# Linear attention and a Mish feed-forward layer: transposes of query features and x moved from TensorE to VectorE and device memory

## The chip, the cores and the metric

The kernel runs on one core of a Trainium2 chip. The metric is device time in microseconds (us) of one execution. The time before the change is 1163.37 us, the median of 3 runs (1163.05 to 1163.79). The profiled execution that all views below show took 1165.86 us, with a span of 1164.1 us between the first and the last instruction.

## What is computed

First comes an attention with positive features, for 8 batches, 8 heads, 576 positions and head size 64. Its result, as 4608 rows of 512, goes through a feed-forward layer with 2048 inner columns.

```python
def phi(x):
    proj = np.einsum('bhsd,df->bhsf', x, w_phi)
    proj = proj - np.max(np.abs(proj), axis=-1, keepdims=True)
    return np.concatenate([np.exp(proj), np.exp(-proj)], axis=-1)
q_p, k_p = (phi(q), phi(k))
kv = np.einsum('bhsf,bhsd->bhfd', k_p, v)
z = np.sum(k_p, axis=2)
num = np.einsum('bhsf,bhfd->bhsd', q_p, kv)
den = np.einsum('bhsf,bhf->bhs', q_p, z)[..., None] + 1e-06
x = (num / den)        # then rows of B*S by columns of H*D
h = x @ w_in
sp = np.where(h > 20.0, h, np.log1p(np.exp(np.minimum(h, 20.0))))
g = h * np.tanh(sp)    # Mish
return (g @ w_out).astype(np.float32)
```

## The kernel before

**The work.** The 4608 rows are 18 chunks `c` of 256. A chunk has two query units `q{c}_{g}` (g = 0, 1: two pairs of heads each), so there are 36 of them. The keys are 36 units `k{n}` of 512 rows, loaded five units ahead of the queries.

A key unit is projected (`project`, L241), which gives two tiles `pp` of 128 positions x 128 features for four blocks; VectorE subtracts the largest absolute value (`centre`, L249: two reductions into `m`, two subtractions into `e[:, 0]`); ScalarE takes the two exponentials (`k_exp`, L289); and TensorE adds features times values into `kvps` (`k_sum`, L294). Positions stand on the partitions there, which is what the sum over positions needs.

A query unit starts the same way, but its product with `kv` sums over features, so features have to stand on the partitions. In `q_turn` (L313) TensorE therefore transposes the centred features of each `j` (0, 1) in four 128x128 blocks into a PSUM tile `dt`, and `q_exp` (L319) reads the exponentials from there. `q_num` (L324) makes the products `num`, `q_divide` (L335) divides them by their last column into `x`, and `q_out` (L345) transposes `x` in four blocks into the PSUM tile `xt`, since the feed-forward layer again needs columns of x on the partitions. `q_high` (L352) and `q_low` (L356) split that into a rounded part `xTh` and a rest `xTl`. So a query unit has twelve 128x128 transposes on TensorE: three groups of four, two in `q_turn` and one in `q_out`.

The feed-forward layer of a chunk has 16 tiles `f` of 128 inner columns. `ff_in` (L366) makes `h` of a tile with 12 matmuls of 256 columns. Two tiles share one PSUM bank; there are two such banks (pool `h`). For each pair of tiles ScalarE applies Mish into `u` and rounds it into `gh` (`mish`, L379; the bank is free once `u` is written), VectorE takes the rest `gl` (L388), and `ff_out` (L401) adds six matmuls of 512 columns per tile into the output tiles `o`, some four tiles behind `ff_in`.

**What sets the order.** `Plan` holds every step as a task with an engine, a key (its due time, counted in tiles `f`), an assumed duration, the tasks that it depends on and the buffers that it takes and gives back. `order` (L57) plays them through and writes down the order in which each engine issues them. On the chip each engine follows that order strictly: an instruction that waits holds up everything behind it on its engine, and so does a DMA that waits on SyncE (SP). From the seventh query unit on (`NFIRST = 6`) a new query unit and a new key unit start every 8 tiles: a *step*. In a step, TensorE does, in this order, the sum of the old key unit and `num` of the old query unit, then `project` of the next query and key unit, among `ff_in` and `ff_out` in turn.

ScalarE computes Exp and Mish from two function tables; each change costs an `ACT_TABLE_LOAD`.

Of the kernel before, what the change touches and what calls it, by code (L numbers as in the profile page):

```python
# [8 lines left out]
F32 = mybir.dt.float32  # L9
# [7 lines left out]
P = 128  # L17
# [5 lines left out]
CH = 256  # L23
# [8 lines left out]
PARTS = ((4, 8, 16), (4, 8, 16))  # L32
NSUMMED = 16

NK, LEAD = B * NHP * S // 512, 5
LEADIN = 5
FIRST_KEYS = {0: -14.0, 1: -13.0, 2: -12.0, 3: -11.0, 4: -10.0, 5: 5.0, 6: 7.0, 7: 9.0, 8: 10.0, 9: 26.0, 10: 30.0}
FIRST_QUERIES = {0: -9.0, 1: -8.0, 2: -2.0, 3: -1.0, 4: 11.0, 5: 12.5}
NFIRST = 6
E0, E1, GX = 0.27, 0.36, 0.6  # L40
WKEYS = [-7.0, -6.0, -5.0, -4.0, -1.5, -0.5, 0.5, 1.5, 3.0, 3.5, 4.0, 4.5, 7.5, 8.0, 8.5, 9.0]
# [4 lines left out]
class Plan:  # L46
# [3 lines left out]

    def add(self, name, engine, key, took, fn, deps=(), take=(), give=(), late=0.15, table=None, size=0):
        task = dict(name=name, engine=engine, key=key, took=took, fn=fn, deps=deps, take=take, give=give, late=late,
                    table=table, size=size, seq=len(self.tasks))
        self.tasks.append(task)
        self.named[name] = task

    def order(self, held):  # L57
# [8 lines left out]

        def ready(task):
            for dep in task["deps"]:
# [52 lines left out]
def attention_then_mish(ctx, tc, qT, kT, va, w_phi, w_in, w_out, out):  # L121
# [39 lines left out]
    def bank(kind, shape, name):  # L161
        return banks[kind].tile(shape, F32, tag=kind, name=name)
# [103 lines left out]
    def halves(ps, lhsT, rhs, start, stop):  # L266

        for h in range(2):
            rows = slice(h * D, (h + 1) * D)
            nc.tensor.matmul(ps[rows], lhsT[:, rows], rhs[h], start=start, stop=stop, skip_group_check=True)  # L270

# [38 lines left out]

    turned, nums, x_live, xT, xt_ps = {}, {}, {}, {}, {}

# [6 lines left out]
    def q_exp(c, g, j):  # L319
        e, ps = features[f"q{c}_{g}"][j], turned.pop((c, g, j))  # L320
        for s in range(2):
            nc.scalar.activation(e[:, s, :], ps, AF.Exp, scale=2.0 * s - 1.0)  # L322

    def q_num(c, g, i):  # L324
        es = features[f"q{c}_{g}"]
        ps = nums[c, g, i] = bank("att", [P, 2, 2, VW], f"num{i}_{c}_{g}")
        for t in range(2):
            r0 = (2 * c + t) * P
            for j in range(2):
                for s in range(2):  # L330
                    halves(ps[:, t, j], es[j][:, s, (2 * i + t) * P:(2 * i + t + 1) * P],
                           [kv[(r0 + h * D) // S, 2 * g + i][:, j, s] for h in range(2)],
                           start=(t == j == s == 0), stop=(s == 1))

    def q_divide(c, g, i):  # L335
        ps = nums.pop((c, g, i))
        if i == 0:
# [5 lines left out]
                                r.unsqueeze(3).broadcast_to([P, 2, 2, D]), op=ALU.mult)  # L343

    def q_out(c, g):  # L345
        x = x_live.pop((c, g))
        ps = xt_ps[c, g] = bank("att", [P, 2, CH], f"xt_{c}_{g}")
        for i in range(2):
            for t in range(2):
                nc.tensor.transpose(ps[:, i, t * P:(t + 1) * P], x[:, i, t], ident)  # L350

    def q_high(c, g):  # L352
        hi = moe.tile([P, 2, CH], F32R, tag="xTh", name=f"xTh_{c}_{g}", bufs=NXT)
        nc.scalar.copy(hi, xt_ps[c, g])  # L354
        xT[c, g] = (hi, None)

    def q_low(c, g):
        hi = xT[c, g][0]
        lo = moe.tile([P, 2, CH], F32R, tag="xTl", name=f"xTl_{c}_{g}", bufs=NXT)
        nc.vector.tensor_sub(lo, xt_ps.pop((c, g)), hi.bitcast(F32))  # L360
        xT[c, g] = (hi, lo)
# [71 lines left out]


    add = plan.add
    key_time = dict(FIRST_KEYS)
    query_time = dict(FIRST_QUERIES)
    for n in range(NFIRST, 2 * NCH):
        query_time[n] = 8.0 * n - 18.0
        if n + LEAD < NK:  # L440
            key_time[n + LEAD] = 8.0 * n - 18.0

    def unit_tasks(unit, t, load, src, kinds, size):
        home, homes = raw_home(), [e_home(), e_home()]
# [5 lines left out]
        for h in homes:  # L450
            last_use.setdefault(h, []).append(f"sum {unit}" if unit[0] == "k" else f"num {unit} 1")
        add(f"project {unit}", "PE", t, 1.0, lambda: project(unit, kinds), deps=[f"load {unit}"],
            take=[(kind, f"pp{j}:{unit}") for j, kind in enumerate(kinds)], give=[token] if half != 0 else [])
# [3 lines left out]
    shared_by, last_use = {}, {}  # L457
    units = sorted([(t, 0, n) for n, t in key_time.items()] + [(t, 1, n) for n, t in query_time.items()])
    for t, is_query, n in units:
        steady = t >= 8.0 * NFIRST - 18.0  # L460
# [3 lines left out]
        sums = t + 7.97 if steady else t + 1.0  # L464
        if not is_query:
            unit = f"k{n}"
            kinds = ("att", "att") if n % 2 or n >= LEADIN else ("h", "h")
            unit_tasks(unit, t + 0.01 * steady, load, kT[n], kinds, 262144)
            for j in range(2):
# [3 lines left out]
            for i in range(4):  # L473
                for p, slot in pairs_of(4 * n + i):
# [6 lines left out]
                    if slot == 4:  # L481
                        last_use.setdefault(spare[1 + NRAWSPARE // 2 + p] if p < NHP else "v", []).append(f"sum {unit}")
                        ends.append(p)
                        give.append(f"v:{p}")
            add(f"sum {unit}", "PE", sums, cost, lambda n=n: k_sum(n), deps=deps, take=take,
                give=give + [f"e{j}:{unit}" for j in range(2)])
# [3 lines left out]
        else:  # L490
            c, g = divmod(n, 2)
            unit = f"q{c}_{g}"
            kinds = (("h", "h") if g else ("att", "att")) if c == 0 else ("h", "att")
            unit_tasks(unit, t + 0.005 * steady, load, qT[c, g], kinds, 262144)
            for j in range(2):
                turn = exps[j] if steady else t + 0.1 + 0.1 * j
                add(f"turn {unit} {j}", "PE", turn, 0.4, lambda c=c, g=g, j=j: q_turn(c, g, j), deps=[f"centre {unit}"],
                    take=[("att", f"dt{j}:{unit}")])
                add(f"exp {unit} {j}", "ACT", turn, 0.94, lambda c=c, g=g, j=j: q_exp(c, g, j), deps=[f"turn {unit} {j}"],
                    give=[f"dt{j}:{unit}"], table="exp")  # L500
            batches = sorted({((2 * c + t2) * P + h * D) // S for t2 in range(2) for h in range(2)})
            lasts = [b for b in batches if (c + 1) * CH >= (b + 1) * S]
            for i in range(2):
                pair = 2 * g + i
                add(f"num {unit} {i}", "PE", sums + 0.01, 0.95, lambda c=c, g=g, i=i: q_num(c, g, i),
                    deps=[f"exp {unit} 0", f"exp {unit} 1"] + [f"kv {b * NHP + pair}" for b in batches],
# [3 lines left out]
                    deps=[f"num {unit} {i}"], take=[] if i else [("half", f"x:{unit}")], give=[f"num{i}:{unit}"])  # L510
            outs = t + 8 + GX if steady else t + 1.2
            add(f"out {unit}", "PE", outs, 0.4, lambda c=c, g=g: q_out(c, g), deps=[f"divide {unit} {i}" for i in range(2)],
                take=[("att", f"xt:{unit}")], give=[f"x:{unit}"])
            add(f"high {unit}", "ACT", outs, 0.48, lambda c=c, g=g: q_high(c, g), deps=[f"out {unit}"], take=[("xT", f"xT:{unit}")])
            add(f"low {unit}", "DVE", outs, 0.6, lambda c=c, g=g: q_low(c, g), deps=[f"high {unit}"], give=[f"xt:{unit}"])

# [93 lines left out]
```

## Time and profile before

| | us |
|---|---|
| median of 3 runs | 1163.37 |
| profiled execution, device time | 1165.86 |
| its span | 1164.1 |
| TensorE matmuls busy in it | 1139.3 |
| VectorE busy | 502.4 |
| ScalarE busy | 679.2 |

PE is TensorE's matmuls, PEld its weight loads, DVE VectorE, ACT ScalarE, SP the engine that issues the DMAs. Matmuls overlap in their pipeline: the time that one really takes from TensorE is the distance from its start to the next one's start, and not the duration that the profile gives. In the timeline a row is one instruction or several equal ones in a row (x4), with its start, its length and, in square brackets, the idle time before it and what ended that.

### The profile page before, as it was taken

To read this page: it belongs to the slowest core of one execution; us is meant where nothing else is said; L and a number is where in the kernel's file an instruction comes from. 1 tells how busy PE (TensorE), PEld (TensorE's weight loads), DVE (VectorE), ACT (ScalarE), POOL (GpSimd) and SP (SyncE) were. 2 spreads that over 40 slices of the span, in tenths; PEclk is the share of its full clock that TensorE was granted. 3 is DMA by queue.
4 is the path that set the end of the run, shared out by engine and by line. 5 is a ranking of instruction groups with operands and counts; after the bars stand their busy time and mean duration, and the time that the engine had idled before them with its cause. 6 is when DMAs were issued, how large, how long until landed. Compare 5 with 4: busy or idle time off the path is not lost.

```text
span 1164.1 us, 26503 instructions
## 1 busy us (share of the span) xinstructions
PE 1139.3 (98%) x11696; PEld 1016.3 (87%) x11696; DVE 502.4 (43%) x1091; ACT 679.2 (58%) x1039; POOL 0.7 (0%) x6
## 2 busy tenths in 40 slices
PE   8998988999999999999999999999999999999998
PEld 7777877899999999899999998999899898888897
DVE  7877989433333333333333333333333342323221
ACT  6678767656655565555555565666665654454422
POOL 0000000000000000000000000000000000000000
PEclk9999999999999999999999999999999999999999
DMA  9811100211011110111111111011101010000000
GB/s 360 338 55 61 43 19 1 61 49 49 19 49 31 32 49 20 49 32 49 31 49 32 49 31 35 17 47 31 49 22 59 19 37 10 29 10 20 1 19 19
DMA packets 25026, 57.67 MB, mean 50 GB/s; under 512 B 2768, under 2 KB 2896, under 8 KB 24912
## 3 DMA queue, kind: packets, MB, share of 16 engines
q1 hardware_dynamic: 24912, 55.98, 14.3%
q8 instruction: 92, 1.51, 0.5%
q14 instruction: 22, 0.18, 0.0%
HBM read 46.53 MB, written 9.44 MB: 48 GB/s over the span
## 4 chain that ended last, share of the span: by engine, by line
PE 84%; DVE 6%; ACT 3%; issue 1%; DVEq 0%; ACTq 0%
PE o L411 33%; PE h L376 32%; PE kvps L270 6%; PE num L270 5%; PE pp_q L247 3%; PE dt L317 2%; PE pp_k L247 2%; PE xt L350 1%; DVE w_out L187 1%; ACT L174 1%; DVE t_out L191 0%; ACT L382 0%; DVE w_in L187 0%; DVE w_out L186 0%; DVE t_out L189 0%
## 5 line engine op out<-in xcount | busy, mean ns | idle before, releaser
L376 PE MATMUL h<-xTh,win 128*128 128x256 f32 x2304 | 466.6, 285 | 5.8 <-ACT u L382 5.7
L376 PEld LDWEIGHTS h<-xTh,win 128*128 128x128 f32 x2304 | 377.1, 190 | 19.5 <-ACT u L382 7.3
L411 PE MATMUL o<-wout,gh 128*128 128x512 f32 x1152 | 371.9, 404 | 0.9 <-DVE part L421 0.9
L376 PE MATMUL h<-xTl,win 128*128 128x256 f32 x1152 | 326.4, 283 | 0.1
L393 DVE TENSOR_TENSOR gl<-u,gh 128x256 fp32r<-128x256 f32 x288 | 111.4, 421 | 427.9 <-ACT gh L385 425.6
L411 PE MATMUL o<-wout,gl 128*128 128x512 f32 x576 | 227.5, 395 | 0.8 <-DVE gl L393 0.8
L411 PEld LDWEIGHTS o<-wout,gh 128*128 128x128 f32 x1152 | 198.0, 189 | 34.2 <-issue 1.1
L376 PEld LDWEIGHTS h<-xTl,win 128*128 128x128 f32 x1152 | 218.8, 190 | 9.1 <-DVE xTl L360 0.3
L354 ACT CAST xTh<-xt 128x512 fp32r<-128x512 f32 x36 | 21.1, 587 | 272.2 <-PE xt L350 272.2
L382 ACT ACTIVATE u<-h 128x512 f32<-128x512 f32 x144 | 86.1, 598 | 112.1 <-PE h L376 111.1
L411 PEld LDWEIGHTS o<-wout,gl 128*128 128x128 f32 x576 | 108.2, 188 | 28.0 <-DVE gl L393 1.6
L382 ACT ACT_TABLE_LOAD x98 | 125.7, 1283 | 1.4
L385 ACT CAST gh<-u 128x256 fp32r<-128x256 f32 x288 | 106.9, 404 | 10.9 <-PE o L411 1.2
L322 ACT ACTIVATE e_q<-dt 128x512 f32<-128x512 f32 x144 | 77.1, 593 | 20.3 <-PE dt L317 19.9
L270 PEld LDWEIGHTS kvps<-v,e_k 128*64 128x64 f32 x2560 | 77.7, 137 | 8.2 <-issue 5.4
L270 PE MATMUL kvps<-v,e_k 128*64 128x66 f32 x2560 | 82.5, 223 | 0.0
L270 PEld LDWEIGHTS num<-kv,e_q 128*64 128x64 f32 x2304 | 70.7, 137 | 8.6 <-issue 7.4
L270 PE MATMUL num<-kv,e_q 128*64 128x66 f32 x2304 | 75.5, 222 | 0.1
L254 DVE TENSOR_REDUCE m_q<-pp_q 128x4 f32<-128x512 f32 x72 | 46.4, 685 | 47.2 <-PE pp_q L247 47.2
L291 ACT ACT_TABLE_LOAD x50 | 64.2, 1283 | 0.9
L340 DVE TENSOR_SCALAR r<-num 128x4 f32<-128x4 f32 x72 | 11.4, 159 | 108.2 <-PE num L270 106.9
L247 PE MATMUL pp_k<-w_phi,raw_k 64*128 64x128 f32 x576 | 44.8, 293 | 8.1 <-DMA raw_k<-kT 4.0
(67 smaller groups left out, 841.3 us busy)
## 6 DMA issues: line engine op xcount, KB each, us to landing
v<-va SPq DMA_DIRECT2D x32, 330.0 KB, 3.0
raw_k<-kT SPq DMA_DIRECT2D x36, 256.0 KB, 2.7
out<-osb SPq DMA_DIRECT2D x36, 256.0 KB, 2.0
raw_q<-qT SPq DMA_DIRECT2D x35, 256.0 KB, 2.9
words_in<-w_in SPq DMA_DIRECT2D x16, 512.0 KB, 9.1
words_out<-w_out SPq DMA_DIRECT2D x16, 512.0 KB, 9.9
raw_k<-qT SPq DMA_DIRECT2D x1, 256.0 KB, 6.1
w_phi<-w_phi SPq DMA_DIRECT2D x1, 64.0 KB, 1.8
```

The source lines that it names most:

```text
L247: nc.tensor.matmul(ps[j][:, n], raw[rows, n * P:(n + 1) * P], w_phi2[rows], start=True, stop=True)
L254: nc.vector.tensor_reduce(ms[j], ps[j], axis=AX.X, op=ALU.max, apply_absolute_value=True)
L270: nc.tensor.matmul(ps[rows], lhsT[:, rows], rhs[h], start=start, stop=stop, skip_group_check=True)
L291: nc.scalar.activation(e[:, 1, :], e[:, 0, :], AF.Exp)
L317: nc.tensor.transpose(ps[:, n * P:(n + 1) * P], e[:, 0, n * P:(n + 1) * P], ident)
L322: nc.scalar.activation(e[:, s, :], ps, AF.Exp, scale=2.0 * s - 1.0)
L354: nc.scalar.copy(hi, xt_ps[c, g])
L376: nc.tensor.matmul(ps, w[:, wcol], x[:, cc % 2, :], start=(n == 0), stop=(n == 11))
L382: nc.scalar.activation(u, h_live.pop((c, fp)).rearrange("p f s -> p (f s)"), AF.Mish)
L385: nc.scalar.copy(gh, u[:, f * CH:(f + 1) * CH])
L393: nc.vector.tensor_sub(gl, u[:, f * CH:(f + 1) * CH], gh.bitcast(F32))
L411: nc.tensor.matmul(ps, g[:, cols], w, start=(i == first and k == 0), stop=(i == end and k == 2))
```

## The change

From the fourth chunk on (`NTURNED = 3`, so 15 of the 18 chunks, 30 query units), `q_turn` and `q_out` on TensorE are gone. In their place stand, three times per unit:

- `regroup` on VectorE: one transpose instruction over 128x512 that turns each 32x32 block in itself, and writes the blocks in another order;
- `send`: a DMA of 256 KB into a buffer `there` in device memory (8 buffers in turn);
- `fetch`: four DMAs of 64 KB that read it back, 32 partitions each, in pieces of 512 bytes, so that whole rows of blocks land on other partitions.

Together these are the full transpose. For the query features the result stands in SBUF, in the same tile, and `q_exp` reads it from there; `q_num` picks its 64 columns from other places, and the queries come from the host with their positions in another order. For x the result stands in the tile of x, and `q_high` and `q_low` read it there with other strides. The first three chunks keep TensorE's transposes.

The plan changes with it: the send is counted as 0.42 us and the four fetches as 1.68 us of SP; a step's due time moves earlier, by up to 2 tiles, over the steps after the fifth (`EARLY`, `RAMP`, `step_time`), so that a unit's sums and products stand up to two tiles sooner among those of the feed-forward layer; `project` of a step may not be issued before the sums and products of the step before (`after`); the exponentials of a query are due somewhat later (`ET`); key unit 10 is due at 28 instead of 30. Exponentials get new neighbours on ScalarE, which changes how often the table is loaded.

```diff
+NTURNED, NTHERE, EARLY, RAMP = 3, 8, 2.0, (5, 4)
...
+    dram = ctx.enter_context(tc.tile_pool(name="dram", bufs=1, space=bass.MemoryType.DRAM))
...
-            nc.tensor.matmul(ps[rows], lhsT[:, rows], rhs[h], start=start, stop=stop, skip_group_check=True)
+            nc.tensor.matmul(ps[rows], lhsT[h], rhs[h], start=start, stop=stop, skip_group_check=True)
+
+    def regroup(src, via):
+
+        nc.vector.transpose(via.rearrange("p (b n j) -> p b n j", b=4, j=32), src.rearrange("p (n b j) -> p b n j", n=4, j=32))
+
+    def send(name, via):
+        there[name] = dram.tile([P, 512], F32, tag="there", name=f"there_{name}", bufs=NTHERE)
+        nc.sync.dma_start(there[name], via)
+
+    def fetch(name, dst):
+        src = there.pop(name)
+        for b in range(4):
+            nc.sync.dma_start(dst[32 * b:32 * b + 32].rearrange("i (a m) -> i a m", a=4),
+                              src[:, b * P:(b + 1) * P].rearrange("(a i) m -> i a m", a=4))
...
     def q_exp(c, g, j):
-        e, ps = features[f"q{c}_{g}"][j], turned.pop((c, g, j))
+        e = features[f"q{c}_{g}"][j]
+        if c >= NTURNED:
+            nc.scalar.activation(e[:, 1, :], e[:, 0, :], AF.Exp)
+            nc.scalar.activation(e[:, 0, :], e[:, 0, :], AF.Exp, scale=-1.0)
+            return
+        ps = turned.pop((c, g, j))
...
+    def q_regroup(c, g, j):
+        e = features[f"q{c}_{g}"][j]
+        regroup(e[:, 0, :], e[:, 1, :])
+
+    def q_send(c, g, j):
+        send(f"e{j}_{c}_{g}", features[f"q{c}_{g}"][j][:, 1, :])
+
+    def q_fetch(c, g, j):
+        fetch(f"e{j}_{c}_{g}", features[f"q{c}_{g}"][j][:, 0, :])
...
+    def x_regroup(c, g):
+        vias[c, g] = work.tile([P, 512], F32, tag="part", name=f"via_{c}_{g}", bufs=NPART)
+        regroup(x_live[c, g].rearrange("p i t m -> p (i t m)"), vias[c, g])
+
+    def x_send(c, g):
+        send(f"x_{c}_{g}", vias.pop((c, g)))
+
+    def x_fetch(c, g):
+        x = x_live.pop((c, g)).rearrange("p i t m -> p (i t m)")
+        fetch(f"x_{c}_{g}", x)
+        xt_ps[c, g] = x.rearrange("p (a n j) -> p n a j", a=4, n=4)
...
+    def step_time(n):
+        return 8.0 * n - 18.0 - EARLY * min(1.0, max(0, n - RAMP[0]) / RAMP[1])
...
+            by_dma = c >= NTURNED
             for j in range(2):
+                if by_dma:
+                    add(f"regroup {unit} {j}", "DVE", t + 0.1, 0.68, lambda c=c, g=g, j=j: q_regroup(c, g, j), deps=[f"centre {unit}"])
+                    add(f"send {unit} {j}", "SP", t + 0.3, 0.42, lambda c=c, g=g, j=j: q_send(c, g, j), deps=[f"regroup {unit} {j}"],
+                        size=262144)
...
```

Where the instructions stand is what the prediction rests on. First TensorE before, in the middle of chunk 11: between a tile of `h` and the tile of `o` that follows stand the four transposes `dt0` of unit q12_1 (j = 0).

```order
L376 MATMUL h_11_8_9109<-xTh_11_1_8760,win_3_2_1862 128x256
L317 MATMUL dt0_12_1_9122<-ident_74,e0_q12_1_9060 128x128 x4
L411 MATMUL o_11_0_0_8938<-wout_4_0_1217,gh0_11_2_8987 128x512 x2
L411 MATMUL o_11_0_0_8938<-wout_4_0_1217,gl0_11_2_9013 128x512
L411 MATMUL o_11_0_1_8939<-wout_4_0_1217,gh0_11_2_8987 128x512 x2
```

After the change no `dt` and no `xt` stands there from chunk 3 on. The sum of key unit k29 and the products of q12_0 now follow each other directly; before the change two tiles of `o` and one of `h` stood between the two.

```order
L275 MATMUL kvps_26_9021<-v_26_8726,e0_k29_8831 64x66 x4
L275 MATMUL kvps_26_9021<-v_26_8726,e1_k29_8833 64x66 x4
L275 MATMUL num0_12_0_9057<-kv_20_6989,e0_q12_0_8797 64x66 x4
L275 MATMUL num0_12_0_9057<-kv_20_6989,e1_q12_0_8799 64x66 x4
L275 MATMUL num0_12_0_9057<-kv_20_6989,e0_q12_0_8797 64x66 x4
```

From the first changed step to the end, the sums and products stand in 46 separate stretches on TensorE before the change, and in 35 after it. 90 groups of four transposes are gone: 53 had a tile of `o` behind them, 37 one of `h`.

Second, ScalarE around the rounding of x of unit q8_1. Before the change:

```order
L354 CAST xTh_8_1_6707<-xt_8_1_6696 128x512
L291 ACT_TABLE_LOAD
L291 ACTIVATE e0_k23_6692<-e0_k23_6692 128x512
L292 ACTIVATE e0_k23_6692<-e0_k23_6692 128x512
L322 ACTIVATE e0_q9_0_6664<-dt0_9_0_6713 128x512 x2
L382 ACT_TABLE_LOAD
L382 ACTIVATE u_7_7_6739<-h_7_14_6621 128x512
```

and after it:

```order
L409 CAST xTh_8_1_6740<-x_8_1_6652 128x512
L310 ACT_TABLE_LOAD
L310 ACTIVATE e0_k23_6734<-e0_k23_6734 128x512
L311 ACTIVATE e0_k23_6734<-e0_k23_6734 128x512
L437 ACT_TABLE_LOAD
L437 ACTIVATE u_7_6_6777<-h_7_12_6657 128x512
```

The exponentials of the query have moved behind the Mish of the next pair, and `u` behind `xTh` is now the pair 7_6 that stands right behind the products on TensorE. In the steps of units 9_0 to 10_1 and of most from 11_1 on, ScalarE takes this `u` directly behind `xTh`, without a table load between, and then four exponentials of the key unit.

Third, SP. Before, the loads around the same step:

```order
L286 DMA v_21_6595<-va 128x660
L239 DMA raw_k24_6658<-kT 128x512
L239 DMA raw_q9_1_6674<-qT 128x512
L432 DMA out<-osb_7_0_6836 128x512
L432 DMA out<-osb_7_1_6844 128x512
```

After, in the units 3_0 to 8_1 (and 11_0), the x of a unit is sent ahead of the next key load, and fetched behind it (from 4_1 on ahead of the query load):

```order
L283 DMA there_x_8_1_6686<-via_8_1_6674 128x512
L244 DMA raw_k24_6698<-kT 128x512
L288 DMA x_8_1_6652<-there_x_8_1_6686 32x4x128 x4
L244 DMA raw_q9_1_6738<-qT 128x512
L283 DMA there_e0_9_0_6765<-e0_q9_0_6704 128x512
```

while in 9_0 to 10_1 and 11_1 to 14_0 the key load, which waits for the projection that frees its buffer, stands ahead of the send:

```order
L305 DMA v_22_6987<-va 128x660
L244 DMA raw_k25_7052<-kT 128x512
L283 DMA there_x_9_0_7062<-via_9_0_7040 128x512
L244 DMA raw_q10_0_7072<-qT 128x512
L288 DMA x_9_0_7008<-there_x_9_0_7062 32x4x128 x4
```

So the send and the fetch of x stand behind loads here that wait for something else than x, and the rest of the queue stands behind both.

More of the change, by code (lines that the diff above doesn't have):

```diff
@@ L49, in __init__, with add @@
         self.rings, self.tasks, self.named = rings, [], {}
-    def add(self, name, engine, key, took, fn, deps=(), take=(), give=(), late=0.15, table=None, size=0):
+    def add(self, name, engine, key, took, fn, deps=(), take=(), give=(), late=0.15, table=None, size=0,
+            after=()):
         task = dict(name=name, engine=engine, key=key, took=took, fn=fn, deps=deps, take=take, give=give, late=late,
-                    table=table, size=size, seq=len(self.tasks))
+                    table=table, size=size, after=after, seq=len(self.tasks))
         self.tasks.append(task)
@@ L67, in ready @@
         def ready(task):
+            if any(dep not in done for dep in task["after"]):
+                return False
             for dep in task["deps"]:
@@ L302, in k_sum @@
                     for s in range(2):
-                        halves(ps[:, j, s], es[j][:, s, i * P:(i + 1) * P], (vt[:, slot, j, :],) * 2,
+                        halves(ps[:, j, s], [es[j][:, s, i * P + h * D:i * P + (h + 1) * D] for h in range(2)], (vt[:, slot, j, :],) * 2,
                                start=(slot == j == s == 0), stop=(slot == 4))
@@ L308, in kv_copy @@
         nc.vector.tensor_copy(kv[p // NHP, p % NHP], kv_ps.pop(p))
-    turned, nums, x_live, xT, xt_ps = {}, {}, {}, {}, {}
+    turned, nums, x_live, xT, xt_ps, there, vias = {}, {}, {}, {}, {}, {}, {}
     def q_turn(c, g, j):
@@ L330, in q_num @@
                 for s in range(2):
-                    halves(ps[:, t, j], es[j][:, s, (2 * i + t) * P:(2 * i + t + 1) * P],
+                    halves(ps[:, t, j], [columns(es[j][:, s, :], t, h) for h in range(2)],
                            [kv[(r0 + h * D) // S, 2 * g + i][:, j, s] for h in range(2)],
@@ L438, in attention_then_mish, with unit_tasks @@
     for n in range(NFIRST, 2 * NCH):
-        query_time[n] = 8.0 * n - 18.0
+        query_time[n] = step_time(n)
         if n + LEAD < NK:
-            key_time[n + LEAD] = 8.0 * n - 18.0
-    def unit_tasks(unit, t, load, src, kinds, size):
+            key_time[n + LEAD] = query_time[n]
+    def unit_tasks(unit, step, t, load, src, kinds, size):
         home, homes = raw_home(), [e_home(), e_home()]
@@ L451, in unit_tasks @@
             last_use.setdefault(h, []).append(f"sum {unit}" if unit[0] == "k" else f"num {unit} 1")
-        add(f"project {unit}", "PE", t, 1.0, lambda: project(unit, kinds), deps=[f"load {unit}"],
+        add(f"project {unit}", "PE", t, 1.0, lambda: project(unit, kinds), deps=[f"load {unit}"], after=sums_at.get(step - 1, ()),
             take=[(kind, f"pp{j}:{unit}") for j, kind in enumerate(kinds)], give=[token] if half != 0 else [])
@@ L467, in attention_then_mish @@
             kinds = ("att", "att") if n % 2 or n >= LEADIN else ("h", "h")
-            unit_tasks(unit, t + 0.01 * steady, load, kT[n], kinds, 262144)
+            unit_tasks(unit, n - LEAD, t + 0.01 * steady, load, kT[n], kinds, 262144)
             for j in range(2):
@@ L484, in attention_then_mish @@
                         give.append(f"v:{p}")
+            if steady:
+                sums_at.setdefault(n if is_query else n - LEAD, []).append(f"sum {unit}")
             add(f"sum {unit}", "PE", sums, cost, lambda n=n: k_sum(n), deps=deps, take=take,
@@ L504, in attention_then_mish @@
                 pair = 2 * g + i
+                if steady:
+                    sums_at.setdefault(n if is_query else n - LEAD, []).append(f"num {unit} {i}")
                 add(f"num {unit} {i}", "PE", sums + 0.01, 0.95, lambda c=c, g=g, i=i: q_num(c, g, i),
```

49 lines of the change are left out of this document (35 added, 14 removed).

## The prediction

> **What bounds the kernel now.** I read the busy times first, then the stretches, then the waits.
>
> ```profile
> PE 1139.3 (98%) x11696; PEld 1016.3 (87%) x11696; DVE 502.4 (43%) x1091; ACT 679.2 (58%) x1039; POOL 0.7 (0%) x6
> ```
>
> By stretch (columns: time, busy time of PE, PEld, DVE, ACT, POOL, then the granted clock, DMA share, GB/s):
>
> ```profile
> 160.00:170.00 10.00, 6.55 (x41) 6.30 (x40) 9.66 (x19) 6.59 (x10) 0.00 (x0) 0.83 0.00 0
> 200.00:300.00 100.00, 99.55 (x1134) 88.87 (x1133) 43.59 (x95) 58.67 (x91) 0.00 (x0) 1.00 0.16 50
> 1000.00:1100.00 100.00, 100.00 (x823) 89.67 (x823) 28.43 (x67) 51.50 (x80) 0.00 (x0) 1.00 0.04 14
> ```
>
> Before 210 us TensorE has holes and VectorE is nearly full (9.66 of 10). After that TensorE has none, with VectorE under 45% and ScalarE at 50 to 60%. The changed units all lie in that second part. So there every microsecond taken from TensorE's queue is a microsecond of the end, as long as no new hole opens. The waits name where a hole would come from:
>
> ```profile
> PE h L376 <- ACT u L382: 5.7, 3, 3.5
> ACT xTh L354 <- PE xt L350: 272.2, 31, 11.2
> ```
>
> TensorE waits for a bank of `h` until ScalarE has read it into `u` (three times, all in the first part), and ScalarE stands idle in front of `xTh` until x is transposed, up to 11.2 us, with `u` queued behind it. That is the place to watch.
>
> **Part by part: what TensorE loses.** TensorE's timeline around one unit (start, length; the time that counts is from start to next start):
>
> ```profile
> 575.82 0.60 PE L350 MATMUL xt<-ident,x 128*128 128x128 f32 x4
> 576.17 0.71 PE L411 MATMUL o<-wout,gh 128*128 128x512 f32 x2
> ...
> 577.66 0.60 PE L317 MATMUL dt<-ident,e_q 128*128 128x128 f32 x4
> 578.01 0.36 PE L376 MATMUL h<-xTh,win 128*128 128x256 f32 x1
> ...
> 579.51 0.62 PE L411 MATMUL o<-wout,gh 128*128 128x512 f32 x2
> ...
> 580.90 0.28 PE L376 MATMUL h<-xTh,win 128*128 128x256 f32 x1
> ...
> 582.32 0.62 PE L411 MATMUL o<-wout,gh 128*128 128x512 f32 x2
> ...
> 583.71 0.28 PE L376 MATMUL h<-xTh,win 128*128 128x256 f32 x1
> ```
>
> A group of four transposes takes 576.17 - 575.82 = 0.35 us. The tile behind it is slower too: `o` behind a group takes 577.66 - 576.17 = 1.49, behind `h` 580.90 - 579.51 = 1.39, so 0.10 more; `h` behind a group 579.51 - 578.01 = 1.50, behind `o` 582.32 - 580.90 = 1.42, so 0.08 more. The order shows 90 such groups gone (30 units x 3), 53 with `o` behind and 37 with `h`: 53 x 0.45 + 37 x 0.43 = **39.8 us**.
>
> The second term is that sums and products now follow each other in 35 stretches instead of 46. What a separate stretch costs:
>
> ```profile
> 565.39 2.09 PE L270 MATMUL kvps<-v,e_k 128*64 128x66 f32 x64
> 567.31 2.05 PE L270 MATMUL num<-kv,e_q 128*64 128x66 f32 x64
> 569.29 0.38 PE L376 MATMUL h<-xTh,win 128*128 128x256 f32 x1
> ...
> ```
> ```profile
> 591.29 2.56 PE L270 MATMUL kvps<-v,e_k 128*64 128x66 f32 x80
> 593.78 0.74 PE L411 MATMUL o<-wout,gh 128*128 128x512 f32 x2
> ...
> 595.29 0.28 PE L376 MATMUL h<-xTh,win 128*128 128x256 f32 x1
> ...
> 596.71 0.62 PE L411 MATMUL o<-wout,gh 128*128 128x512 f32 x2
> ...
> 598.18 2.09 PE L270 MATMUL num<-kv,e_q 128*64 128x66 f32 x64
> 600.21 0.38 PE L376 MATMUL h<-xTh,win 128*128 128x256 f32 x1
> ```
>
> `o` behind `kvps` takes 1.51 (+0.12), `o` ahead of `num` 1.47 (+0.08), `num` behind `o` 2.03 instead of 1.98 (+0.05), and `kvps` ahead of `o` 2.49 for 80, where 64 ahead of `num` take 1.92 and 16 more at 0.03 would make 2.40 (+0.09). Together 0.34; times 11, **3.7 us**. Sum: 43.5 us off TensorE's queue; the rest of its work is unchanged.
>
> **What is added, and who waits for it.** VectorE gets three instructions per unit, SP three sends and twelve fetches. Their prices are not in the trace; the nearest rows:
>
> ```profile
> L429 DVE COPY osb<-o 128x512 f32<-128x512 f32 x31 | 21.3, 688 | 22.1 <-PE o L411 22.1
> L189 DVE TENSOR_SCALAR t_in<-w_in 128x512 uint32<-128x512 uint32 x16 | 6.8, 427 | 0.5
> out<-osb SPq DMA_DIRECT2D x36, 256.0 KB, 2.0
> w_phi<-w_phi SPq DMA_DIRECT2D x1, 64.0 KB, 1.8
> 603.05 0.34 SPq L239 DMA_DIRECT2D raw_k<-kT  x1
> ```
>
> A transpose over 128x512: between 0.43 and 0.69, at the most twice that, 1.4; I take 0.69, as it reorders and does no packed arithmetic. Thirty units x 3 x 0.69 = 62 us more on VectorE, 7% of the part where it is idle over half the time. A send: like `out`, 2.0 us from issue to landing. A fetch: four issues of 0.34, the last landing 1.8 us after its issue like `w_phi` (64 KB, also 512 bytes per partition): 3 x 0.34 + 1.8 = 2.8, and 4 x 1.8 = 7.2 if the four do not overlap at all. [...]
>
> Now the path of x, counted from the mark at which TensorE starts the first `h` behind `num` (569.29 above; before the change).
>
> ```profile
> 569.81 0.42 DVE L342 TENSOR_TENSOR x<-num,r 128x256 f32<-128x256 f32 x1
> ...
> 572.09 1.29 DVE L254 TENSOR_REDUCE m_q<-pp_q 128x4 f32<-128x512 f32 x2 [1.86 <-PE pp_q L247]
> ...
> 577.07 0.69 DVE L360 TENSOR_TENSOR xTl<-xt,xTh 128x512 fp32r<-128x512 f32 x1
> ```
> ```profile
> 576.45 0.59 ACT L354 CAST xTh<-xt 128x512 fp32r<-128x512 f32 x1 [10.78 <-PE xt L350]
> 577.06 1.28 ACT L291 ACT_TABLE_LOAD   x1
> ...
> 579.55 1.07 ACT L322 ACTIVATE e_q<-dt 128x512 f32<-128x512 f32 x2
> 580.63 1.28 ACT L382 ACT_TABLE_LOAD   x1
> 581.92 0.60 ACT L382 ACTIVATE u<-h 128x512 f32<-128x512 f32 x1
> 582.55 0.71 ACT L385 CAST gh<-u 128x256 fp32r<-128x256 f32 x2
> 583.28 1.28 ACT L291 ACT_TABLE_LOAD   x1
> ```
>
> After the change, x is divided at 0.94, turned at 1.6, sent 2.0, fetched 2.8, with three hand-overs at 0.2 (`xTh` began 0.28 behind the end of the `xt` slot, 576.17): ScalarE can start `xTh` at about 7.0. Today it does at 576.45 - 569.29 = 7.2. So the path is no later than today's, and only its price is uncertain.
>
> How late may it be? In the steps up to 8_1, ScalarE then does table, two exponentials, table, `u`: today's 581.92 - 576.45 less the two exponentials of the query (1.08), so `u` starts 4.4 behind `xTh` and ends 5.0 behind it. TensorE needs its bank at the fifth `h`: 583.71 - 569.29 = 14.4 today, less two groups at 0.45, 13.5. So x may come at 8.5; **1.5 us spare**. From 9_0 on, SP holds the send behind a key load that waits for the projection: 603.05 - 600.21 = 2.8, plus 0.34, then 2.0 and 2.8 and hand-overs, 8.3. There `u` follows `xTh` directly, and the second `u` is the tight one: 0.6 + 0.6 + 0.7 + 2.5 + 1.2 + 1.1 + 1.3 + 0.6 = 8.6 behind the start of `xTh`, needed four tiles later at 19.1: x may come at 10.5; **2.2 us spare**. Behind the waiting `xTh` on ScalarE stand these very instructions; behind the waiting fetch on SP stand query loads and stores, due a step later. The features take 577.07 - 569.29 = 7.8, plus 0.7, 2.0, 2.8, 0.6: 13.9, where ScalarE wants them at about 14.0, and the `u` behind them has 2 us left.
>
> So I book no stall in the regular steps, and 1 us (0 to 3) for the first changed unit, whose fetch stands behind two stores that wait for the end of chunk 2. The sum is 43.5 - 1 = 42.5: the profiled execution goes from 1165.86 to 1123.4, and the median, 2.5 lower, from 1163.37 to **1120.9 us**. ScalarE's table loads fall from 196 to 164 by the order; not on the path.
>
> **The rivals.**
>
> *Slower: x comes back too late in each step.* If the four fetches run one after the other (7.2), x comes 4.4 us later: 2.9 past the first limit and 2.2 past the second, in 30 steps some 75 us, so 1196. Holes also cost clock: in 160 to 170 us, where the one long hole of 3.5 us lies, the mean clock was 0.83, which is 3.4 us at half speed, 1.7 us lost; with that in every step, 1247. It decides from 43/30 = 1.4 us past the limits, a round trip some 3 us longer than my 5.5. For it: no row has a read behind a write, and both margins are small. Against: `out` and `w_phi` are the same forms, and DMA share is 0.04 to 0.16. The Trainium skill (VectorE: DVE Perf Modes, Rules for kernel authors) advises TensorE for a 128x128 transpose where PSUM will do, which speaks for this rival; it does not weigh which engine is full.
>
> *Less gained.* The slow-downs behind the groups might belong to the alternation itself and stay: then 90 x 0.35 = 31.5, 1131.9. Or the spare time is overdrawn by half a microsecond in most steps: 15 us, 1136. Against the first: `o` behind `h` at 1.39 is in the trace wherever nothing stands between.
>
> *No gain:* VectorE becomes the bound. It would need some 6 us per transpose to fill its idle 60 us in 100 (about ten transposes in 100 us); unlikely.
>
> **How the numbers follow.** Forecast 0.70; less gained 0.17; slower 0.09; no gain 0.02; more gained, by holes of the first part that close, 0.02. A difference of 0.2% is about what a measurement of this kernel can tell from none. Faster 0.89, same 0.02, slower 0.09. The range goes from 1117 (no stall at the first unit, and 3 us for the terms' rounding) to 1136 (the second case) and leaves out the last three.
>
> **What would show it.** Right: no `dt` or `xt` after the third chunk, `o` at 1.39 and `h` at 1.42 in nearly all places, TensorE at 100% in every stretch from 210 us on, the steps 1.4 us shorter, and `xTh` starting 7 us behind the mark. Wrong: rows in which `h` waits for `u`, or `num` for the exponentials, once per step, with clock below 1.00; or transposes on VectorE above 1.4 us, or fetches landing later than 4 us.

## The result and the profile after

| | before | after |
|---|---|---|
| median, us | 1163.58 (1163.05 to 1165.53, 4 runs) | **1131.1** (1129.5 to 1132.4, 4 runs) |
| profiled execution, us | 1165.86 | 1130.25 |
| its span, us | 1164.1 | 1128.5 |
| from the first changed unit's projection to the end of the span, us | 1164.1 - 208.0 = 956.1 | 1128.5 - 206.5 = 922.0 |

The ratio is 0.9717 [0.9699, 0.9736]: 32.5 us less, where 42.5 were forecast. The time lies inside the range and 10 us above the forecast.

The busy line of the profile after:

```profile
PE 1096.4 (97%) x11336; PEld 974.0 (86%) x11336; DVE 555.3 (49%) x1181; ACT 640.7 (57%) x1007; POOL 0.7 (0%) x6
```

TensorE has 360 matmuls less (30 units x 12 transposes), and VectorE rises by 53 us to 49%, far from a bound. The two stretches of 100 us were shown for before; the three of 10 us hold the largest holes behind the first changed unit (columns as there):

```profile
200.00:300.00 100.00, 98.55 (x1115) 87.54 (x1114) 51.39 (x107) 59.72 (x91) 0.00 (x0) 1.00 0.35 107
...
1000.00:1100.00 100.00, 99.91 (x801) 89.19 (x801) 31.61 (x74) 36.04 (x69) 0.00 (x0) 1.00 0.15 48
...
410.00:420.00 10.00, 8.89 (x58) 7.74 (x57) 4.01 (x8) 6.57 (x9) 0.00 (x0) 1.00 0.50 152
470.00:480.00 10.00, 9.38 (x59) 8.10 (x58) 3.48 (x7) 7.58 (x10) 0.00 (x0) 1.00 0.53 155
595.00:605.00 10.00, 8.26 (x53) 7.12 (x52) 1.39 (x4) 9.76 (x15) 0.00 (x0) 1.00 0.14 41
```

TensorE is no longer at 100% everywhere. In three places of 10 us it stands still for 0.6 to 1.7 us, at a granted clock of 1.00. The waits, and the prices that the prediction had to estimate (waits, then groups of VectorE, then DMA issues):

```profile
ACT xTh L409 <- DMA x<-there_x: 295.7, 28, 14.8
...
PE h L431 <- ACT u L437: 10.6, 10, 3.5
...
PE num L275 <- ACT e_q L342: 1.3, 2, 0.7
```
```profile
L279 DVE STREAM_TRANSPOSE e_q<-e_q 128x512 f32<-128x512 f32 x60 | 38.8, 684 | 0.0
...
L279 DVE STREAM_TRANSPOSE via<-x 128x512 f32<-128x512 f32 x30 | 21.3, 712 | 1.0
```
```profile
there_x<-via SPq DMA_DIRECT2D x30, 256.0 KB, 2.0
x<-there_x SPq DMA_DIRECT2D x120, 64.0 KB, 2.0
```

TensorE now waits ten times for `u`, where it waited three times before (5.7 us, all in the first part). The seven new waits are where most of the holes lie. A transpose takes 0.68 to 0.71 us, as estimated, and the median send 2.0 us. But medians are not what a step with 1.5 us to spare depends on. This is the worst step, whose mark (first `h` behind `num`) is at 580.0: SP, then ScalarE, then TensorE.

```profile
582.88 0.34 SPq L244 DMA_DIRECT2D raw_k<-kT  x1
583.31 0.38 SPq L283 DMA_DIRECT2D there_x<-via  x1
...
588.91 1.92 SPq L288 DMA_DIRECT2D x<-there_x  x4
```
```profile
592.68 0.62 ACT L409 CAST xTh<-x 128x512 fp32r<-128x512 f32 x1 [14.83 <-DMA x<-there_x]
593.21 0.59 ACT L437 ACTIVATE u<-h 128x512 f32<-128x512 f32 x1
...
600.83 0.60 ACT L437 ACTIVATE u<-h 128x512 f32<-128x512 f32 x1
```
```profile
598.20 0.62 PE L466 MATMUL o<-wout,gh 128*128 128x512 f32 x2
...
601.48 0.38 PE L431 MATMUL h<-xTh,win 128*128 128x256 f32 x1 [1.74 <-ACT u L437]
...
603.00 0.62 PE L466 MATMUL o<-wout,gh 128*128 128x512 f32 x2
...
604.39 0.28 PE L431 MATMUL h<-xTh,win 128*128 128x256 f32 x1
```

The send of x is issued straight behind a key load of 256 KB. Its fetch is issued 588.91 - 583.31 = 5.6 us later, where 2.0 were booked for the send. So `xTh` starts 592.68 - 580.0 = 12.7 behind the mark (limit of the prediction: 10.5). The second `u` ends at 601.43, 21.4 behind it (limit: 19.1), and TensorE stands: the slot of `o` takes 601.48 - 598.20 = 3.28 us instead of 1.39, which the next `o` takes again (604.39 - 603.00). That is 1.89 us more, where the row of the wait has 1.74; so holes are measured on the slots.

**The account.** Each slot of TensorE's order (start to next start) is compared with the shortest slot of its kind; what it has above that is a *hole* (single holes are good to about 0.1 us). In the 922.0 us after there are 10.4 us of holes: 1.6 around the `num` of the first changed unit (223.8 to 228.0), 7.5 in ten places in the steps up to 893 us, and 1.3 in the last steps. Without holes 911.6 are left, 44.5 below the 956.1 of before, which has none there. So the work term, 43.5, holds, and the 10 us that are missing are holes.

Three theories followed. A: the work term is right, and holes behind the round trip of x take the rest. B: the slow-downs behind the groups partly stay, so the work term is too large. C: what VectorE and the DMAs now do beside TensorE slows its own instructions.

### The profile page after: what moved, and what is told of

Its sections match the earlier page's. It is cut to its first block, busy times and chain, and to the rows that moved or that the text cites. A ratio compares the mean times of both kernels' runs of the same rounds, so it can differ in the third digit from the quotient of the medians.

```text
span 1128.5 us, 26884 instructions
## 1 busy us (share of the span) xinstructions
PE 1096.4 (97%) x11336; PEld 974.0 (86%) x11336; DVE 555.3 (49%) x1181; ACT 640.7 (57%) x1007; POOL 0.7 (0%) x6
## 4 chain that ended last, share of the span: by engine, by line
PE 66%; ACT 8%; DVE 8%; DMA 6%; SPq 3%; issue 2%; ACTq 0%; DVEq 0%
PE h L431 26%; PE o L466 26%; PE kvps L275 5%; PE num L275 5%; DMA there_x<-via 3%; SPq L288 3%; PE pp_q L252 2%; ACT L437 2%; DMA e_q<-there_e 2%; PE pp_k L252 1%; DMA x<-there_x 1%; ACT u L437 1%; ACT L310 1%; DMA there_e<-e_q 1%; ACT e_q L341 1%
## 5 line engine op out<-in xcount | busy, mean ns | idle before, releaser
L431 PE MATMUL h<-xTh,win 128*128 128x256 f32 x2304 | 464.0, 284 | 11.1 <-ACT u L437 10.6
L466 PE MATMUL o<-wout,gh 128*128 128x512 f32 x1152 | 365.1, 398 | 1.0 <-DVE part L476 1.0
L409 ACT CAST xTh<-x 128x512 fp32r<-128x512 f32 x30 | 18.6, 621 | 314.1 <-DMA x<-there_x 295.7
L440 ACT CAST gh<-u 128x256 fp32r<-128x256 f32 x288 | 103.4, 404 | 7.6 <-PE o L466 2.3
L310 ACT ACTIVATE e_k<-e_k 128x512 f32<-128x512 f32 x72 | 45.1, 626 | 9.6 <-DVE e_k L267 9.1
```

Source lines behind the costliest of these rows:

```text
L310: nc.scalar.activation(e[:, 1, :], e[:, 0, :], AF.Exp)
L409: nc.scalar.copy(natural(hi), xt_ps[c, g])
L431: nc.tensor.matmul(ps, w[:, wcol], x[:, cc % 2, :], start=(n == 0), stop=(n == 11))
L440: nc.scalar.copy(gh, u[:, f * CH:(f + 1) * CH])
L466: nc.tensor.matmul(ps, g[:, cols], w, start=(i == first and k == 0), stop=(i == end and k == 2))
```

## The experiments

**1. No round trip (noturn).** From the fourth chunk on, transposes on VectorE, sends and fetches are left out, so the features and x are not transposed there; plan and TensorE's order stay.

```diff
     def q_regroup(c, g, j):
...
-        regroup(e[:, 0, :], e[:, 1, :])
+        return
...
     def q_send(c, g, j):
-        send(f"e{j}_{c}_{g}", features[f"q{c}_{g}"][j][:, 1, :])
+        return
```

(The same in `q_fetch`, `x_regroup`, `x_send`, and the call of `fetch` in `x_fetch`.)

> This kernel keeps the changed kernel's plan and TensorE's order to the last instruction, but from the fourth chunk on it leaves out the transposes altogether: no VectorE transpose, no send, no fetch, so features and x stay untransposed. Theory A (the 10 us of holes on TensorE in the changed kernel's profile come from x and features coming back late from device memory): all holes after 210 us go, 1131.1 - 10.4 = 1120.7 us (1119 to 1122.5). Rival B (they come from the new order on ScalarE itself, exponentials and table loads ahead of u): the holes stay, 1129 to 1132. Rival C (the DMA traffic slows TensorE's own rows): more than 1.5 us below 1119.

Measured: 1120.49 us (1118.85 to 1121.89), ratio 0.962 [0.9604, 0.9636]. A stretch of this run, which stands for all from 210 us on:

```profile
400.00:500.00 100.00, 100.00 (x1083) 90.75 (x1079) 39.43 (x89) 60.20 (x87) 0.00 (x0) 1.00 0.13 40
```

No hole is left, and the time is what the prediction gave for no stall. Slot by slot, in the same order of TensorE, the changed kernel takes 10.2 us more than this one from 206 us on. So the holes come with the round trips, and B and C fall. Whether those of x or those of the features bring them, this run cannot tell, since both are left out; experiment 3 can.

**2. The loads behind the fetch of x (xfirst).** A key or query load now waits for the fetch of x two steps before its own step, so that the send of x has no load ahead of it.

```diff
-        add(f"load {unit}", "SP", load, 0.42, lambda: load_raw(unit, home, src), take=take, size=size)
+        behind = [f"out q{(step - 2) // 2}_{step % 2}"] if step - 2 >= 2 * NTURNED else []
+        add(f"load {unit}", "SP", load, 0.42, lambda: load_raw(unit, home, src), deps=behind, take=take, size=size)
```

> One edit: a key or query load may stand on SP only behind the fetch of the x of its step, so that x's send and fetch follow each other with nothing between. TensorE's order is the same, instruction for instruction. Theory A1 (x is late because loads of 256 KB stand ahead of it on SP and in the DMA queue): xTh starts at 7.0 to 7.6 us behind the mark in every regular step, instead of 7.6 and 9.8; the holes fall from 10.4 us to 2 to 4; 1123 to 1125 us. Rival A2 (x is late by instruction loads that share the DMA engines, whatever stands in the queue): the late ones stay in some steps, 1127 to 1130. Rival B (ScalarE's order): no change, 1131.

Measured: 1133.06 us (1132.09 to 1136.44), ratio 0.9735 [0.9717, 0.9752]: a miss, no better than the changed kernel. Its waits:

```profile
PE h L431 <- ACT u L437: 13.0, 11, 3.5
```

In the steps from 9_0 on, `xTh` moved from 9.7 to 10.7 behind the mark to mostly 7.1 to 7.6, as expected, and the holes of the middle steps fell from 7.5 to about 3.3 us. But the loads now stand ahead of the *features'* sends. In the last steps, where a step is shorter, the features come back 12.9 to 14.4 behind the mark instead of 11.3 to 13.1, the second `u` ends at 18.7 to 20.1 (limit there: about 18.1), and the holes grow from 1.3 to 6.3 us. The load was only pushed in front of another send.

**3. Only the features take the new way (featonly).** x is transposed by TensorE as before.

```diff
+X_BY_DMA = False
...
-            if by_dma:
+            if by_dma and X_BY_DMA:
                 add(f"regroup {unit}", "DVE", sums + 0.1, 0.68, lambda c=c, g=g: x_regroup(c, g),
```

(The same condition in the line that gives the buffer of x back.)

> Only the query features go by VectorE and device memory; x of all chunks is transposed by TensorE as before the change. 30 groups of four transposes stay on TensorE, 13.5 us by their rows. Theory A (x's way back is what comes late): holes of 1 to 3 us, 1131.1 - 10.4 + 13.5 + 2 = 1136 us (1134 to 1138). Rival (the features come late, and ScalarE waits for them in front of u): the holes stay at 10, 1144 us.

Measured: 1136.28 us (1135.48 to 1139.0), ratio 0.9761 [0.9746, 0.9776]. Holes: 2.3 us, 1.7 of them at the first changed unit. So the middle and last holes come with the round trip of x; that of the features alone opens almost none.

**4. The new plan with TensorE's transposes (turned18).**

```diff
-NTURNED, NTHERE, EARLY, RAMP = 3, 8, 2.0, (5, 4)
+NTURNED, NTHERE, EARLY, RAMP = 18, 8, 2.0, (5, 4)
```

> The plan of the change (earlier steps, order of projects, later exponentials) with TensorE's transposes in all chunks. By TensorE's order, 32 stretches of sums and products instead of 46, so 4.7 us less work: theory (the plan alone opens no holes and is worth only the stretches) 1158.9 us (1157 to 1161). Rival (the holes belong to the new plan): 1165 to 1170. Rival (a good part of the gain is the plan's): below 1150.

Measured: 1159.55 us (1158.48 to 1161.13), ratio 0.9958 [0.9943, 0.9973], no holes. The plan alone brings 4 to 5 us. Its sums and products stand in 32 stretches instead of 46, and 14 x 0.34 = 4.8.

**5. The changed kernel again (after_again).** No edit; it stands beside 6 to 8 on the same chip.

> The changed kernel itself once more, on the chip on which the next three run, as their yardstick: 1131 us (1129.5 to 1132.5), with 8 to 12 us of holes after 210 us.

Measured: 1129.65 us (1128.09 to 1131.84), ratio 0.9702 [0.9689, 0.9716], with 11.7 us of holes.

**6. The loads behind both round trips (loadslast).** A load waits for the features' last fetch of the step before.

```diff
-        add(f"load {unit}", "SP", load, 0.42, lambda: load_raw(unit, home, src), take=take, size=size)
+        behind = [f"turn q{(step - 1) // 2}_{(step - 1) % 2} 1"] if step - 1 >= 2 * NTURNED else []
+        add(f"load {unit}", "SP", load, 0.42, lambda: load_raw(unit, home, src), deps=behind, take=take, size=size)
```

> One edit: a key or query load may stand on SP only behind the fetch of the features of its step, so behind x's and the features' whole round trip. TensorE's and ScalarE's orders stay the same. Theory A1 (what stands ahead on SP and in the DMA queue makes x and the features late): holes of 1.6 us at the first unit, about 3 us in the middle steps as with the loads behind x alone, and about 1 us instead of 6 in the last ones: 1126 to 1127 us. Rival (the late steps have another cause than the loads): 1131 to 1133, as with the loads behind x alone.

Measured: 1125.41 us (1123.27 to 1128.72), ratio 0.9667 [0.9648, 0.9686]: 4.2 us below the changed kernel beside it. Its waits, in an execution of 1127.09:

```profile
PE h L431 <- ACT u L437: 8.3, 8, 3.5
```

Holes: 6.3 us, of which 1.8 lie at the first unit, 2.7 in the middle and 1.8 in one of the last steps. So the loads ahead of the sends cost about what was expected. In the three steps with the largest holes outside the first unit (1.3, 0.8 and 1.8 us), the send of x still landed 3.7 to 4.3 us after its issue, with no key or query load ahead of it (in two of them a load of `v` was issued 2.3 and 2.8 us before); more on these below.

**7. Loads last, Mish ahead of the key's exponentials, stores behind the first fetch (best).** On top of 6, a key's exponentials may not be issued before a given pair of Mish, so that in every step `u` follows `xTh` directly, with no table change between the two; and the two stores of chunk 2 that stood ahead of the first changed unit's fetch go behind it.

```diff
+                tile = 8 * (n - LEAD) - 20
-                add(f"exp {unit} {j}", "ACT", exps[j], 0.94, lambda n=n, j=j: k_exp(n, j), deps=[f"centre {unit}"], table="exp")
+                add(f"exp {unit} {j}", "ACT", exps[j], 0.94, lambda n=n, j=j: k_exp(n, j), deps=[f"centre {unit}"], table="exp",
+                    after=[f"mish {tile // 16} {tile % 16 // 2}"] if tile // 16 >= 3 else ())
...
                     add(f"store {c} {tt}", "SP", when + 0.02, 0.42, lambda c=c, tt=tt: store(c, tt), deps=[f"evict {c} {f} {tt}"],
+                        after=["turn q3_0 1"] if c == 2 else (),
```

> Three edits: the loads behind the features' fetch, as in the kernel before; the exponentials of a key unit may stand on ScalarE only behind the Mish of the pair that follows the products, so that u stands right behind xTh in all steps (table loads 140 instead of 164); and the stores of chunk 2 stand behind the fetch of the first changed unit's features. TensorE's order is the same. If the limits are as worked out (x may come at 8.5 us behind the mark where exponentials stand between xTh and u, at about 10 where u follows at once), the late round trips of up to 2 us no longer reach TensorE: holes of 0 to 2 us, 1121 to 1123 us. Rival (each late round trip costs, wherever u stands): 1125 to 1127.

Measured: 1120.98 us (1118.52 to 1121.37, 5 runs), ratio 0.9622 [0.9609, 0.9635]. It beats both kernels, and it equals the kernel without any round trip (noturn). Its holes are 1.1 us; two stretches, and SP in the step that was the worst of the changed kernel:

```profile
400.00:500.00 100.00, 100.00 (x1061) 90.74 (x1056) 47.30 (x102) 52.76 (x84) 0.00 (x0) 1.00 0.29 92
600.00:700.00 100.00, 100.00 (x1138) 91.19 (x1135) 48.94 (x105) 49.91 (x81) 0.00 (x0) 1.00 0.29 92
```
```profile
576.65 0.33 SPq L283 DMA_DIRECT2D there_x<-via  x1
578.76 1.99 SPq L288 DMA_DIRECT2D x<-there_x  x4
583.25 0.93 SPq L283 DMA_DIRECT2D there_e<-e_q  x2
585.42 3.64 SPq L288 DMA_DIRECT2D e_q<-there_e  x8
589.17 0.37 SPq L244 DMA_DIRECT2D raw_k<-kT  x1
```

The fetch is issued 2.1 us behind the send instead of 5.6, and the key load comes last.

How much of the gain over loadslast belongs to Mish going first is not shown. The two sends of x that were late there (4.3 us in unit 6_0, 3.7 in 7_0) landed after 2.4 and 2.2 us here, and after 2.2 and 2.4 in the kernel of experiment 10, so by the limits the holes behind them would have gone in any order on ScalarE. In the steps up to 8_1, x came past the limit of 8.5 only in 4_1 (8.6 here, 8.9 in experiment 10). There the first `u` ended at 9.8 and 10.0 and no hole opened, where the changed kernel, with x at 8.8, had one of 0.6.

**8. x makes the way twice (twice).** On top of 6, x is sent, read back into the same buffer and sent again, so that it comes 4.5 to 5 us later in most steps. This brings the slower rival about.

```diff
     def x_send(c, g):
+        send(f"first_{c}_{g}", vias[c, g])
+        nc.sync.dma_start(vias[c, g], there.pop(f"first_{c}_{g}"))
         send(f"x_{c}_{g}", vias.pop((c, g)))
```

> Loads last, and x goes to device memory twice: sent, read back as it is into the same buffer by one DMA, sent again, then fetched. That makes x later by about 2.9 + 2.0 + 0.2 = 5.1 us, at 12.3 behind the mark. Theory (limits at 8.5, at about 10, and at about 8.3 in the last steps): holes of about 3.8 us in 12 steps, 2.2 in 11 and 4 in 5, some 90 us: 1120.5 + 1.6 + 90 = 1212 us; if each hole also brings 3.4 us of half clock, 27 x 1.7 more: 1258. Rival (the limits are softer, since ScalarE idles later in a step): under 1160.

Measured: 1260.22 us (1260.2 to 1260.24, 2 runs), ratio 1.0822 [1.0803, 1.0842]. A wait and a stretch of it:

```profile
PE h L433 <- ACT u L439: 93.3, 40, 5.2
```
```profile
1000.00:1100.00 100.00, 87.45 (x731) 77.02 (x730) 31.68 (x71) 39.85 (x65) 0.00 (x0) 0.90 0.25 79
```

`xTh` comes 11.7 to 13.0 behind the mark in 25 of the 30 steps, 13.7 to 14.6 in four, and 8.5 in one. From the first changed unit to the end it takes 1258.4 - 205.1 = 1053.3 us, 141.7 above the 911.6 that loadslast has without its holes. The waits for `u` are 93.3 - 5.7 = 88 of that. The mean clock is 0.962, where loadslast has 0.995: 1258.4 x 0.038 = 48 us of clock lost against 1125.3 x 0.005 = 6. The two together are 130 of the 141.7. So the second price of the slower rival, holes that cost clock as well, is real.

**9. No earlier due times (early0).**

```diff
-NTURNED, NTHERE, EARLY, RAMP = 3, 8, 2.0, (5, 4)
+NTURNED, NTHERE, EARLY, RAMP = 3, 8, 0.0, (5, 4)
```

> The changed kernel with EARLY at 0: a step is due as early among the feed-forward tiles as before the change, so x of a chunk's second half is wanted 10.8 us behind the mark (x rounded and its rest, for the first h of the chunk) instead of 13.5. By TensorE's rows its order has 47 separate stretches and 6.2 us more work. Theory (only the sum and the margins count): x is rounded and its rest taken at 9.0 to 11.2, so every second step is late by 0 to 0.5 us, and u stands behind xTh with a later limit: 1120.5 + 6.2 + 1.6 + 1 to 6 = 1129 to 1134 us. Rival (the early steps are what makes the round trip possible at all): over 1140.

Measured: 1150.02 us (1149.14 to 1150.98), ratio 0.9875 [0.9862, 0.9889]; what I held likely (1129 to 1134) failed, and the rival (over 1140) holds. Its waits:

```profile
PE h L431 <- DVE xTl L415: 7.9, 7, 1.9
PE h L431 <- ACT u L437: 7.2, 7, 3.5
...
PE o L466 <- ACT gh L440: 2.7, 3, 1.6
```

A wait stands here that the changed kernel does not have: `h` of a new chunk comes before its own `xTl` is ready. Holes are 24.4 us, 14.0 more, and without them the stretch takes 940.5 - 24.4 = 916.1, 4.5 us more work (6.2 were expected). Starting the steps up to two tiles sooner is part of what makes the round trip affordable.

**10. As best, but with the stores where they were (bfirst).**

```diff
-                        after=["turn q3_0 1"] if c == 2 else (),
```

> The best kernel so far without its third edit: the stores of chunk 2 stand ahead of the fetch of the first changed unit's features again. Theory (that fetch is late only because SP waits for the stores' data): the 1.6 us of holes at the first unit come back, and nothing else, 1122.6 us (1121 to 1124). Rival (the second edit had removed them): 1121.

Measured: 1123.77 us (1121.74 to 1123.88, 5 runs), ratio 0.9646 [0.9632, 0.9659]. Holes are 3.6 us, 1.6 of them back at the first changed unit, and 1.4 behind one late send of x in the last steps (4.3 us, unit 16_0), where best has 0.7. So the fetch behind the two stores costs about what was booked for it.

One table of the profiled executions holds the ledger. "Stretch" goes from the first changed unit's projection to the end of the span (us):

| kernel | stretch | holes | without them |
|---|---|---|---|
| before | 956.1 | 0 | 956.1 |
| turned18 | 951.1 | 0 | 951.1 |
| featonly | 927.2 | 2.3 | 924.9 |
| after | 922.0 | 10.4 | 911.6 |
| after_again | 923.4 | 11.7 | 911.7 |
| xfirst | 922.8 | 11.1 | 911.7 |
| loadslast | 917.9 | 6.3 | 911.6 |
| bfirst | 915.2 | 3.6 | 911.6 |
| best | 912.8 | 1.1 | 911.7 |
| noturn | 911.7 | 0 | 911.7 |

The last column falls in steps: 5.0 with the plan, 26.2 with the 60 groups of the features, 13.2 with the 30 groups of x. Everything else is holes. One part is hidden in the second step: turned18 has 32 stretches of sums and products, featonly and all below it have 35, and three stretches at 0.34 are 1.0 us.

## Why the prediction was right in direction and 10 us too low

**TensorE's work: right.** Worked out: 39.8 for 90 groups and 3.7 for fewer stretches. Measured: 26.2 + 13.2 = 39.4, and 5.0 with the plan; 44.4 in all. With the 1.0 of the three stretches put where it belongs, it is 40.4 for the groups (0.45 each) and 4.0 for the stretches. That the tile behind a group takes 0.08 to 0.10 less once the group is gone is shown too: `o` between two `h` takes 1.39 in the median of the changed kernel's 176 such slots, and 90 x 0.35 would have been 31.5. The Trainium skill (VectorE: DVE Perf Modes, Rules for kernel authors) advises TensorE for such a transpose if the result may go to PSUM; here moving 360 of them off the full engine takes some 40 us from it, at 60 us of an engine that is not full.

**The first changed unit: right.** Booked 1 (0 to 3); measured 1.6, taken away in best and back in bfirst.

**The prices: two right, one short.** VectorE's transpose 0.69: 0.68 and 0.71. A send 2.0: 2.0 where nothing stands ahead of it. A fetch 2.8: 3.3 in clean steps, because the four issues stand about 0.44 apart, not 0.34, and the last lands 2.0 behind its own, not 1.8. The Trainium skill (DMA: Bandwidth & Descriptors, Anatomy of one DMA) fits a DMA that GpSimd issues with about 2.0 us plus its bytes at 436 GB/s. Carried over to these, which SyncE issues, that gives as an estimate 2.6 for the send, where the trace has 2.0, and 3.2 for the fetch with issues 0.34 apart, where it has 3.3.

**The margins: right.** The limits named for `u` are those at which holes begin. In the steps from 4_0 to 8_1, a first `u` that ended 12.3 to 13.2 behind the mark left under 0.1 us, and those at 13.6, 14.0, 14.3 and 14.8 left 0.3, 0.6, 0.9 and 1.4 us (worked out: 13.5). From 9_0 on, second `u` at 19.0 or less left nothing, and those at 19.3, 19.5, 19.7 and 21.4 left 0.3, 0.5, 0.7 and 2.0 (worked out: 19.1).

**What failed** is the step "So I book no stall in the regular steps". I set clean rows, 2.0 and 2.8, against margins of 1.5 and 2.2 us, as if each transfer took its median, although the text itself had the send stand behind a key load from 9_0 on. Directly behind that load a send landed after 3.0 to 3.5 us, not 2.0; `xTh` started at 9.7 to 10.7 there instead of 8.3, so those steps just met their limit of 10.5, and whatever else came late opened a hole: the worst step (2.4 in two slots, its send landing after 5.5), one at 10.7 (0.5), and 14_0, in which the features came back at 15.9 instead of 13.9 (0.3). In 11_0, which has no key load in front of x, the features at 15.0 were enough for 0.7. In the steps up to 8_1 no key load is in front, and the holes (3.5 us) lie where single transfers were slow: sends of 3.8 and 4.3, fetches of 4.2 to 5.0. With 1.3 in the last steps that is 8.8 us. Without any round trip they are gone (noturn), with the loads last they are halved (loadslast), and in best 0.7 and a few tenths are left, in part because fewer sends were late there.

**The rivals.** The second form of "less gained" (spare time overdrawn in most steps, 1136) named what happened, though in fewer steps and by more in each. Its first form, slow-downs that stay, gives 1131.9, nearly the measured number, but falls by noturn and by the ledger: a number that fits is not a cause. The slower rival was not entered, since the four fetches overlap (3.3, not 7.2); twice shows that such a delay costs about what it said, with half clock: 141.7 us for 4.5 to 5 us, where 75 and 51 were booked for 4.4, and 42 of them clock. The point from which it would decide was not tried. VectorE never came near a bound: 51% at most in these stretches.

## What to carry to other kernels

Price a new hand-over by what stands ahead of it in its queue, and compare the spread of such transfers, not their median, with the spare time. When a change lands between forecast and rival, add up the holes on the full engine slot by slot: what is left is the work term, and it tells which of the two was wrong. A latency that is needed within a step goes first in the queue, and bulk loads that are due a step later go last (4.2 us here by that alone, 8.7 with the two further edits of best).

## What was not expected of the hardware

The program's own instructions are loaded by the same DMA engines. The profile after counts these packets, and the landing times of the DMAs to and from the buffer of x, 30 sends and 120 fetches together (minimum, median, maximum; the 5.5 is the send of the worst step):

```profile
q8 instruction: 89, 1.46, 0.5%
```
```profile
DMA to landing us min/median/max: 1.8/2.0/5.5
```

By the trace's packets each is 16 KB and takes 0.9 to 1.9 us, one about every 12 us. In the kernel best, the 77 sends that had no such packet from 0.5 us before to 2 us behind their issue landed after 2.06 us in the median and 2.46 at most. Of the 13 that had one, 9 landed after 2.0 to 2.5 and 4 after 3.5 to 4.2. In the changed kernel the two large holes at 415.8 and 475.3 us follow sends that met one at 406.5 (1.86 us) and 466.0 (1.42), and the worst step above met one at 585.7 (0.96) behind its key load. Before the change there were as many of these packets (92), but the last key or query load ahead of a projection was issued at least 26 us before it, and from 210 us on nothing waited.

When the packet starts sets the late ones apart. Take the eight profiles with a round trip other than twice, and in them the sends that had no key or query load still on its way. All 25 with a packet that started 0.4 to 1.6 us behind their issue landed after 2.9 to 4.5 us. Of the 479 with none from 1 us before to 2 us behind, the median is 2.07, and two took more than 3. A load of `v` on its way does not do it: the sends of x in 5_0 and 8_0 had one in after, after_again, xfirst and loadslast and landed after 2.0 to 2.7, while 12_1 in xfirst and bfirst and 16_0 in loadslast and bfirst had none and landed after 4.1 to 4.3. This is a coincidence in eight profiles, not a shown cause: no run moved or removed the instruction loads. What the runs do show is that with the loads last and Mish first, the steps up to 14_1 have no hole above 0.2 us; one late send in the last steps of best still cost 0.7 us.

The second surprise is the clock. The holes of the changed kernel behind its first changed unit, up to 2 us, cost none: it is 1.00 in every stretch shown above for that kernel. In twice, three stretches that begin at a slot with a hole of 3.45, 3.46 and 3.82 us (measured as above):

```profile
303.00:315.00 12.00, 8.71 (x44) 7.29 (x43) 2.21 (x5) 11.74 (x16) 0.00 (x0) 0.86 0.35 103
548.00:560.00 12.00, 8.70 (x56) 7.57 (x55) 2.21 (x5) 11.74 (x16) 0.00 (x0) 1.00 0.34 105
581.00:593.00 12.00, 8.36 (x35) 7.16 (x35) 2.21 (x5) 11.74 (x16) 0.00 (x0) 0.72 0.36 112
```

Of two holes of the same size the one costs 0.14 x 12 = 1.7 us of clock, as the single hole of 3.5 us before did, and the other none; the third costs 3.4. And a shorter one can cost as much. In early0 TensorE stands idle for 1.95 us ahead of an `h`, and in the 12 us around it the mean clock is 0.86 (a row of the timeline and a stretch):

```profile
575.57 0.46 PE L431 MATMUL h<-xTl,win 128*128 128x256 f32 x1 [1.95 <-DVE xTl L415]
...
570.00:582.00 12.00, 9.95 (x47) 8.26 (x45) 3.19 (x6) 9.11 (x14) 0.00 (x0) 0.86 0.37 120
```

So in these traces the length of a hole does not tell what it costs in clock: 1.95 us cost 1.7 here, where 1.9 in the changed kernel and 3.46 in twice cost nothing. What else decides stays open. Where it strikes, it adds 1.7 to 3.4 us to the hole.
